# Dilated and sliding-window attention before a fused feed-forward: w3 turned by VectorE, dilated v loaded in place, gates in pairs

## The chip, the cores and the metric

The kernel runs on one core of a Trainium2 chip. The metric is device time in microseconds (us) of one execution, the median of three. The engines are TensorE (PE; its weight loads are shown as PEld), VectorE (DVE), ScalarE (ACT), GpSimd (POOL) and SyncE (SP). GpSimd and SyncE here mostly issue DMA transfers.

## What is computed

q, k and v have 8 batches of 8 heads, 576 positions and 64 columns, in float32. Heads 0 to 3 attend to the last 32 positions, heads 4 to 7 to every fourth of the last 128. The 4,608 rows of 512 columns that result go through a feed-forward with a product in the middle:

```python
mask_plain = (rel >= 0) & (rel < 32)
mask_dil = (rel >= 0) & (rel < 128) & (rel % 4 == 0)
scores = np.where(masks, scale * q @ k.T, -1e9)      # masks: plain for heads 0..3
attn = softmax(scores); x = attn @ v                 # x: (4608, 512)
a = x @ w1; b = x @ w2                               # (4608, 1024)
out = ((a * b) @ w3) @ w_out                         # (4608, 512)
```

The maximum is not subtracted in the kernel. All matrix products take bf16 operands.

## The kernel before

**The fused weight.** (a*b) @ w3 @ w_out is computed as (a*b) @ wf with wf = w3 @ w_out, made once. For the product, each block of 128 rows of w3 (`load_w3`, L323) is turned: eight TensorE transposes of 128x128 (`w3_back`, L644), a copy from PSUM to SBUF by ScalarE (`w3_keep`, L652), eight matmuls with w_out (`w3_mul`, L656), and a cast into `wf_sb` (`w3_done`, L668).

**Attention.** A batch is done in two halves of heads, u = 0 (plain) and u = 1 (dilated), each in six blocks of 96 positions. The dilated heads become the plain pattern by putting positions of equal remainder modulo 4 behind each other, in the order of `RES`. q and k are loaded with a cast to bf16 (`load_rows`, L247) and turned by VectorE's 32x32 transposes of 4-byte words (`turn`, L377). A `Group` (L426) computes the scores of up to five blocks of 4 heads (40 matmuls), ScalarE takes the exponential (L465), VectorE multiplies by the mask (L473). For batches below `BIASED` a group has three blocks, and four matmuls with the identity first add a bias of -30000 outside the window (L437), in place of the mask. A `Step` (L475) multiplies by v with a column of ones (`values`, L482), takes the reciprocal of the ones column (L501) and normalizes (`norm`, L503: one instruction for u = 0, two for u = 1). For batches below `TURNED` TensorE turns the result (`back`, L527) and ScalarE or VectorE copies it to `XT` (`keep`, L536); later batches use a DMA transpose issued by SP.

v must lie with positions on partitions, each block with a halo of 32 earlier positions. For batches 0 and 1 it is turned by VectorE and again by TensorE (`v_back`, L407) and put away by ScalarE or VectorE (`v_keep`, L417). From batch 2 on (`DIRECT_V`) it is loaded in place: the plain heads by one DMA (L286), the dilated ones by eight in rows of 64 numbers, 256 bytes (`load_v_dil`, L291); the halo is copied by VectorE (`halo_v`, L305).

**Feed-forward.** The rows are taken in 16 units of 288. For each unit and each of the 8 blocks f of d_ff, `up` (L559) makes a and b with four matmuls each, `copy_a` (L571) brings a to SBUF by ScalarE, `gate` (L576) multiplies by VectorE into `gt`, a ring of four units. `down` (L585) multiplies 128 rows of the ring by `wf_sb`; `copy_y` and `store` write them out. Thus a `down` needs all eight parts of wf, and unit 4 needs room in the ring.

**The order of the work.** Every step is a `Task` with an engine, an assumed duration, its inputs and a priority (`RANK`, `FIRST`; smaller goes first). `Plan.run` (L80) plays these through in Python, gives every PSUM user one, two or four of the eight banks, and fills empty TensorE time before the first `up` with dummy matmuls (`fill`, L700). The result is a fixed order for each engine; on the chip, each instruction waits for its inputs. The loads form one queue on GpSimd, with at most eight in flight: k, q of batch 0, heads 0 to 3, come by SP in float32 (`load_whole`, L256), then the lists `B0_LOADS` and `FIRST_LOADS` (L40, L45) in their order. In these, "w" is a part of w1 and w2, "3" a block of w3, "o" a half of w_out, and the digits give the part or batch and the half of the heads. `HALVED` and `ON_DVE` say which copies go to which engine; `begin` (L1001) orders the first two units, half of f at a time.

Of the kernel before, what the change touches and what calls it, by code (L numbers as in the profile page):

```python
# [10 lines left out]
P = 128  # L11
# [18 lines left out]
BIASED = 1  # L30
LATE = False
TURNED = 2
# [3 lines left out]
RANK = dict(E=0.5, VK=3, K=2, N=0.2, T=0.5, VT=0.05, S=0.1, V=0.05, X=0.1, W=0.5, C=5)  # L36
FIRST = {"E": 3, "VK": 1, "K": 0.2, "N": 2, "T": 0.2, "VT": 0.05, "S": 0.3, "V": 0.1, "X": 0.3}
WARM = 25
FILL = 110
FIRST_LOADS = ("30", "w0", "v10", "w1", "w2", "31", "k10", "q10", "o0", "o1", "32", "33", "34", "q11", "k11", "v11", "35", "36", "37")  # L40
SHIFT = {}
ON_DVE = ("K0.2", "VK0.1.1", "W3D1", "W3D4", "W3D5")
GRP = 5
WHOLE = ("qn", "kn")
B0_LOADS = ("v0", "q1", "k1", "v1")  # L45
HALVED = ("K0.0", "K0.1", "K0.3", "K1.1", "VK0.0.0", "VK0.1.0", "VK1.0.1", "VK1.1.0")
MASK_AT = 19.5
PARTED = 0
BUSY = 4500
LEAD = 1.1  # L50
# [13 lines left out]
class Plan:  # L64
# [15 lines left out]
    def run(self):  # L80
# [42 lines left out]
        while len(order) < n:  # L123
            progress = True
            while progress:
                progress = False
                for e in engines:
# [8 lines left out]
                    else:  # L136
                        idle = e == "PE" and now >= self.fill_from and self.fill_to.start is None
                        f = Task("fill", "PE", FILL, [], self.fill, 0, 1, 0, ())
# [48 lines left out]
def kernel(  # L187
# [28 lines left out]
    w3_pool = ctx.enter_context(tc.tile_pool(name="w3", bufs=7))  # L216
# [9 lines left out]
        const.tile([P, 2 * B, 2, VC], BF16, name="XT1"),  # L226
# [4 lines left out]
    vps = [const.tile([P, H, 6, PITCH], BF16, name=f"vp{i}") for i in range(2)]  # L231
# [4 lines left out]
    vts = [const.tile([P, 2, PADK + S, 2], BF16, name=f"vt{i}") for i in range(1)]  # L236
# [47 lines left out]
    def load_v_plain(b):  # L284
        flat = vps[b % 2][:, 0:4, :, :].rearrange("p h m e -> p (h m) e")
        nc.gpsimd.dma_start(  # L286
            out=flat[32:P, :, 0:D],
            in_=v_rows(b, 0, 0, [[D, QB], [QB * D, 24], [1, D]]),
        )

    def load_v_dil(b, m):  # L291
        vp = vps[b % 2]
        (r, r2), mu = RES[2 * (m // 3) : 2 * (m // 3) + 2], m % 3
        runs = {
            0: [(0, 96, r, 0)],
            1: [(0, 48, r, 96), (48, 48, r2, 0)],
            2: [(0, 96, r2, 48)],
        }[mu]
        for p0, n, res, t0 in runs:
            nc.gpsimd.dma_start(  # L300
                out=vp[32 + p0 : 32 + p0 + n, 4:8, m, 0:D],
                in_=v_rows(b, 4, 4 * t0 + res, [[4 * D, n], [S * D, 4], [1, D]]),
            )
# [10 lines left out]
    def load_wo(c):  # L314
        g = slice(4 * c, 4 * c + 4)
        nc.gpsimd.dma_start(
            out=wo_sb[:, g, :],
            in_=moe_w_out[512 * c : 512 * (c + 1), :].rearrange("(a p) f -> p a f", p=P),
        )
# [3 lines left out]
    def load_w3(ft):  # L323
        w3n[ft] = w3_pool.tile([P, d_ff], BF16, tag="w3", name="w3n")
        nc.gpsimd.dma_start(out=w3n[ft], in_=moe_w3[ft * P : (ft + 1) * P, :])
# [91 lines left out]
    def v_keep(b, u, half, eng, hs=slice(0, 4)):  # L417
        dst = vps[b % 2][:, 4 * u : 4 * u + 4, 3 * half : 3 * half + 3, 0:D]
# [56 lines left out]
    class Step:  # L475


        def __init__(self, b, u, hf, parts):
            self.b, self.u, self.hf, self.parts = b, u, hf, parts
            self.o = [None, None]  # L480

        def values(self):  # L482
# [3 lines left out]
            self.o = o[:, :, 0 : 3 * (D + 1)].rearrange("p h (m e) -> p h m e", m=3)  # L486
            for g in range(4):
                for mm, (grp, i) in enumerate(self.parts):
                    c0 = (grp.n * g + i) * QB
                    nc.tensor.matmul(  # L490
                        out=self.o[:, g, mm, :],
                        lhsT=grp.et[:, c0 : c0 + P],
                        rhs=vps[self.b % 2][:, 4 * self.u + g, 3 * self.hf + mm, 0 : D + 1],
                        start=True,
                        stop=True,
                    )

        def recip(self):
            self.rcp = wk_pool.tile([P, 4, 3], F32, tag="rcp", bufs=4, name="rcp")
            self.xo = wk_pool.tile([P, 12 * D], BF16, tag="xo", bufs=4, name="xo")  # L500
            nc.vector.reciprocal(out=self.rcp[0:QB, :, :], in_=self.o[0:QB, :, :, D])  # L501

        def norm(self, part):  # L503

            if part is None:
                hs = slice(0, 4)
                dst = self.xo[0:QB, :].rearrange("p (m g d) -> p g m d", m=3, g=4)
            else:
                hs = slice(2 * part, 2 * part + 2)
                dst = self.xo[0:QB, :].rearrange("p (q m g d) -> p q g m d", q=2, m=3, g=2)  # L510
                dst = dst[:, part, :, :, :]
            n = hs.stop - hs.start
            nc.vector.tensor_tensor(  # L513
                out=dst,
                in0=self.o[0:QB, hs, :, 0:D],
                in1=self.rcp[0:QB, hs, :].unsqueeze(3).to_broadcast([QB, n, 3, D]),
# [3 lines left out]
        def cols(self):  # L520

            if self.u == 0:
                m0 = self.b * BLK + 3 * self.hf
                return XT[0][:, m0 : m0 + 3, :, :].rearrange("p m g x -> p (m g x)")
            return XT[1][:, 2 * self.b + self.hf, :, :].rearrange("p g x -> p (g x)")
# [26 lines left out]
    def unit_cols(k, c):  # L552

        b, hf = k // 2, k % 2
        if c < 2:
            return XT[0][:, b * BLK : (b + 1) * BLK, c, 48 * hf : 48 * hf + 48]
        return XT[1][:, k, c - 2, :].rearrange("p (r m t) -> p m r t", r=2, m=BLK)

    def up(k, f, key, chunks=ORDER, first=True, last=True):  # L559
        if first:  # L560
            held[(key, k, f)] = bank(UNIT)
        for j, c in enumerate(chunks):
            nc.tensor.matmul(  # L563
                out=held[(key, k, f)],
                lhsT={"a": w1_sb, "b": w2_sb}[key][:, c, f * P : (f + 1) * P],
                rhs=unit_cols(k, c),
                start=(first and j == 0),
                stop=(last and j == len(chunks) - 1),
            )

    def copy_a(k, f):  # L571
        a_sb = wk_pool.tile([P, UNIT], BF16, tag="asb", bufs=6, name="asb")
        nc.scalar.copy(out=a_sb, in_=held[("a", k, f)])  # L573
        held[("s", k, f)] = a_sb

    def gate(k, f):  # L576
        c0 = (k * UNIT) % RING
        nc.vector.tensor_tensor(  # L578
            out=gt[:, f, c0 : c0 + UNIT].rearrange("p (r m t) -> p m r t", r=2, m=BLK),
            in0=held[("b", k, f)].rearrange("p (m r t) -> p m r t", r=2, m=BLK),  # L580
            in1=held[("s", k, f)].rearrange("p (m r t) -> p m r t", r=2, m=BLK),
# [61 lines left out]

    def w3_back(ft):  # L644
        x = bank(KFF * P, BF16).rearrange("p (g x) -> p g x", g=KFF)
        for g in range(KFF):
            nc.tensor.transpose(  # L647
                out=x[:, g, :], in_=w3n[ft][:, g * P : (g + 1) * P], identity=ident
            )
# [6 lines left out]
    def w3_mul(ft):  # L656
        o = bank(d_model)
        for g in range(KFF):
            nc.tensor.matmul(  # L659
                out=o,  # L660
                lhsT=w3T[ft][:, g, :],
# [28 lines left out]
    def constants():  # L690
        for t in kts + vts:
            nc.vector.memset(t[:, :, 0:PADK, :], 0.0)
        for t in ets:
            for x in (4 * VC, 4 * GRP * QB):
                nc.vector.memset(t[:, x : x + 32], 0.0)
        for t in vps:
# [33 lines left out]
    def loads_v(b):  # L730
        old = vdone.get(b - 2, [])
        LV[b] = [load(f"LP{b}", 1300, 4700, old, lambda: load_v_plain(b))]
        LV[b] += [
            load(f"LD{b}.{m}", 600 if m % 3 != 1 else 1200, 770, old, lambda m=m: load_v_dil(b, m))
            for m in range(6)
# [316 lines left out]
```

## Time and profile before

| | |
|---|---|
| median of 3 runs | 254.95 us (254.93 to 254.96) |
| span of the profiled execution, first to last instruction | 253.2 us |
| around the span (difference to the median) | 1.75 us |
| TensorE busy | 245.8 us |
| VectorE busy | 167.9 us, 350 instructions |
| ScalarE busy | 124.3 us |
| chain of waits, share of TensorE | 90% |
| first product of `up` in the chain | 20.44 us |
| last matmul product of `down` starts | 247.76 us |
| mean granted TensorE clock | 0.998 |

The profile comes from one execution. Matmuls overlap, so the mean time of one matmul in the groups is longer than its share of TensorE; that share is read from the chain of waits, where 12 products of `up` follow each other in 1.47 us. A group's line gives the source line, engine, operation, output and input tiles, shape, count, then busy time, mean ns of one, and the idle time of the engine just before, with what ended it. The profile gives no separate time for the profiled execution beyond its span.

### The profile page before, as it was taken

The page shows a single profiled execution, that of the slowest core. Times are in us where ns is not written, and L with a number is a line of the kernel's source. Part 1 is how long each engine was busy: PE and PEld are TensorE (multiplying, and loading weights), DVE is VectorE, ACT ScalarE, POOL GpSimd, SP SyncE. Part 2 cuts the span into 40 slices and gives each one's busy share as a digit, 9 for nine tenths or more (in the row PEclk, how much of TensorE's full clock was granted, in tenths as well). Part 3 has the DMA queues.
Part 4 walks back from the last instruction along what each step waited for, and adds up shares of the span by engine and source line. Part 5 has one row for each costly group of instructions (what it writes and reads, how often), then busy time and mean ns, then how long its engine had stood idle before and what let it go on. Part 6 is the DMA issues. An engine that isn't in the chain of part 4 may idle for free.

```text
span 253.2 us, 6818 instructions
## 1 busy us (share of the span) xinstructions
PE 245.8 (97%) x2760; PEld 170.6 (67%) x2760; DVE 167.9 (66%) x350; ACT 124.3 (49%) x221; POOL 67.8 (27%) x106
## 2 busy tenths in 40 slices
PE   7889999999999999999999999999999999999994
PEld 5668876565767676677676766676767666777662
DVE  3998657697898887588868977837737365333321
ACT  5664555766635534362626526356353643333331
POOL 7635835343614432303250310800000000000000
PEclk9999999999999999999999999999999999999999
DMA  7999999999997999998799667862332223311114
GB/s 226 204 200 209 207 210 211 208 107 184 220 168 121 189 170 208 235 95 114 122 202 110 89 77 104 137 84 65 67 65 67 67 67 67 104 36 51 41 41 124
DMA packets 59422, 33.40 MB, mean 132 GB/s; under 512 B 44800, under 2 KB 49280, under 8 KB 59392
## 3 DMA queue, kind: packets, MB, share of 16 engines
q0 software_dynamic: 38592, 18.81, 58.7%
q1 hardware_dynamic: 20656, 14.10, 24.3%
q8 instruction: 21, 0.34, 0.6%
q14 instruction: 9, 0.07, 0.1%
q10 hardware_dynamic: 144, 0.07, 0.1%
HBM read 38.80 MB, written 9.44 MB: 190 GB/s over the span
## 4 chain that ended last, share of the span: by engine, by line
PE 90%; DVE 5%; DMA 2%; issue 1%; ACT 1%; ACTq 0%; DVEq 0%
PE ps L563 49%; PE ps L589 24%; PE ps L659 6%; PE ps L490 4%; PE ps L454 4%; DMA gt<-in_q_dram 2%; DVE qt L403 1%; DVE xo L513 1%; PE ps L647 1%; PE ps L607 1%; PE ps L701 1%; PE ps L530 1%; ACT qn L278 0%; DVE et L473 0%; PE ps L412 0%
## 5 line engine op out<-in xcount | busy, mean ns | idle before, releaser
L563 PE MATMUL ps<-XT,w_sb 128*128 128x288 bf16 x1024 | 136.3, 286 | 0.0
L563 PEld LDWEIGHTS <-w_sb 128*128 128x128 bf16 x1024 | 97.8, 98 | 30.6
L578 DVE TENSOR_TENSOR gt<-ps,asb 128x288 bf16<-128x288 f32 x128 | 57.5, 454 | 49.0 <-PE ps L563 46.7
L573 ACT CAST asb<-ps 128x288 bf16<-128x288 f32 x128 | 50.7, 398 | 49.3 <-PE ps L563 46.0
L589 PE MATMUL ps<-wf_sb,gt 128*128 128x512 bf16 x280 | 65.8, 379 | 0.0
L600 ACT COPY osb<-ps 128x512 f32<-128x512 f32 x35 | 20.5, 585 | 55.1 <-PE ps L589 55.0
L589 PEld LDWEIGHTS <-gt 128*128 128x128 bf16 x280 | 27.2, 98 | 26.9
L300 POOL DMA_DIRECT2D vp<-in_v_dram x48 | 30.3, 639 | 48.3 <-PE ps L490 30.3
L465 ACT ACTIVATE et<-ps 128x1920 bf16<-128x1920 f32 (+2 forms) x21 | 34.2, 1633 | 7.7 <-PE ps L454 5.5
L513 DVE TENSOR_TENSOR xo<-ps,rcp 96x384 bf16<-96x384 f32 (+1 forms) x48 | 31.4, 675 | 0.5
L473 DVE TENSOR_TENSOR et<-et,mask 128x960 bf16<-128x960 bf16 (+1 forms) x34 | 21.2, 645 | 6.8 <-ACT et L465 6.7
L403 DVE STREAM_TRANSPOSE qt<-qn 128x320 uint32<-128x320 uint32 (+3 forms) x34 | 22.3, 670 | 2.1 <-ACT qn L278 1.8
L490 PEld LDWEIGHTS <-et 128*128 128x128 bf16 x384 | 14.6, 98 | 1.9 <-issue 0.4
L490 PE MATMUL ps<-vp,et 128*128 128x65 bf16 x384 | 15.5, 193 | 0.1
L659 PE MATMUL ps<-wo_sb,w3T 128*128 128x512 bf16 x64 | 15.0, 379 | 0.1
L403 DVE STREAM_TRANSPOSE kt<-kn 128x320 uint32<-128x320 uint32 (+3 forms) x18 | 11.6, 646 | 4.5 <-PE ps L454 4.3
L454 PEld LDWEIGHTS <-kt 32*128 32x128 bf16 x768 | 9.1, 92 | 5.9 <-issue 4.7
L454 PE MATMUL ps<-qt,kt 32*128 32x96 bf16 x768 | 12.1, 201 | 0.7 <-DVE kt L388 0.7
L501 DVE RECIPROCAL rcp<-ps 96x12 f32<-96x12 f32 x32 | 6.9, 218 | 8.3 <-PE ps L490 8.0
L286 POOL DMA_DIRECT2D vp<-in_v_dram x6 | 7.2, 1194 | 11.5 <-PE ps L490 10.7
L659 PEld LDWEIGHTS <-w3T 128*128 128x128 bf16 x64 | 5.9, 98 | 6.3 <-issue 0.3
L388 DVE STREAM_TRANSPOSE kt<-kn 128x576 uint32<-128x576 uint32 (+1 forms) x9 | 9.9, 1121 | 0.2 <-PE ps L454 0.2
(56 smaller groups left out, 117.6 us busy)
## 6 DMA issues: line engine op xcount, KB each, us to landing
qn<-in_q_dram POOLq DMA_DIRECT2D x6, 576.0 KB, 8.2
kn<-in_k_dram POOLq DMA_DIRECT2D x6, 576.0 KB, 9.0
w3n<-in_moe_w_dram POOLq DMA_DIRECT2D x8, 256.0 KB, 11.2
out_dram<-osb SPq DMA_DIRECT2D x7, 256.0 KB, 3.0
out_dram<-osb SPq DMA_DIRECT2D x8, 224.0 KB, 2.9
vp<-in_v_dram POOLq DMA_DIRECT2D x6, 288.0 KB, 9.2
out_dram<-osb SPq DMA_DIRECT2D x8, 192.0 KB, 2.9
out_dram<-osb SPq DMA_DIRECT2D x8, 160.0 KB, 3.2
```

Source lines behind the costliest of these rows:

```text
L300: nc.gpsimd.dma_start(out=vp[32 + p0 : 32 + p0 + n, 4:8, m, 0:D], in_=v_rows(b, 4, 4 * t0 + res, [[4 * D, n], [S * D, 4], [1, D]]),)
L403: nc.vector.transpose(out=o, in_=i)
L454: nc.tensor.matmul(out=self.sp[:, g, QB * i : QB * i + QB], lhsT=kt[prt, u, QB * m : QB * m + P, c], rhs=qq, start=(c == 0 and not biased) ...
L465: nc.scalar.activation(out=ev, in_=self.sp[:, :, 0:x], func=ACT.Exp, scale=scale)
L473: nc.vector.tensor_tensor(out=ev, in0=ev, in1=mk, op=AL.mult)
L490: nc.tensor.matmul(out=self.o[:, g, mm, :], lhsT=grp.et[:, c0 : c0 + P], rhs=vps[self.b % 2][:, 4 * self.u + g, 3 * self.hf + mm, 0 : D + ...
L513: nc.vector.tensor_tensor(out=dst, in0=self.o[0:QB, hs, :, 0:D], in1=self.rcp[0:QB, hs, :].unsqueeze(3).to_broadcast([QB, n, 3, D]), op=AL ...
L563: nc.tensor.matmul(out=held[(key, k, f)], lhsT={"a": w1_sb, "b": w2_sb}[key][:, c, f * P : (f + 1) * P], rhs=unit_cols(k, c), start=(first ...
L573: nc.scalar.copy(out=a_sb, in_=held[("a", k, f)])
L578: nc.vector.tensor_tensor(out=gt[:, f, c0 : c0 + UNIT].rearrange("p (r m t) -> p m r t", r=2, m=BLK), in0=held[("b", k, f)].rearrange("p ( ...
L589: nc.tensor.matmul(out=y, lhsT=gt[:, f, c0 : c0 + P], rhs=wf_sb[:, f, :], start=(f == 0), stop=(f == KFF - 1),)
L659: nc.tensor.matmul(out=o, lhsT=w3T[ft][:, g, :], rhs=wo_sb[:, g, :], start=(g == 0), stop=(g == KFF - 1),)
```

## The change

- w3 is loaded in four pieces of 256 rows; each piece by four DMAs of 256 columns into 32 partitions each (`load_w3`), in rows of 1,024 bytes. VectorE turns it by one transposing instruction of 512 words for each 128 rows (`w3_turn`); `w3_back` and `w3_keep` are no longer used (`W3_DVE` names all four pieces). `w3_mul` reads every second element of the turned tile. `w_out` is loaded with another assignment of rows to partitions to match.
- v of the dilated heads is loaded in place for all batches, in rows of two positions (128 numbers, 512 bytes), by four DMAs, into tiles `vds` of their own. One row serves two remainders; the first has its ones column ahead of it, the second behind. `halo_v` covers the plain heads only.
- Blocks f are taken in pairs after the first ten (`SINGLE`): `up`, `copy_a` and `gate` work on two neighbouring banks.
- `norm` is one instruction for all heads; `XT` has one layout for both halves.
- `BIASED` is 2 instead of 1. Ranks, the order of the loads (w_out and w3 last), which copies go to which engine, the place of the masks (`MASK_AT`) and `LEAD` are changed. The dummy matmuls are limited to 200.

```diff
-BIASED = 1
+BIASED = 2
+W3_DVE = (0, 1, 2, 3)
+SINGLE = 10
-RANK = dict(E=0.5, VK=3, K=2, N=0.2, T=0.5, VT=0.05, S=0.1, V=0.05, X=0.1, W=0.5, C=5)
-FIRST = {"E": 3, "VK": 1, "K": 0.2, "N": 2, "T": 0.2, "VT": 0.05, "S": 0.3, "V": 0.1, "X": 0.3}
+RANK = dict(E=14.678, VK=10.289, K=0.115, N=1.309, T=1.47, VT=1.262, S=3.624, V=0.444, X=8.99, W=0.183, C=2.862)
+FIRST = dict(E=3.06, VK=0.542, K=2.149, N=1.723, T=5.596, VT=64.744, S=0.678, V=0.475, X=11.212)
-FIRST_LOADS = ("30", "w0", "v10", "w1", "w2", "31", "k10", "q10", "o0", "o1", "32", "33", "34", "q11", "k11", "v11", "35", "36", "37")
+FIRST_LOADS = ('k01', 'v00', 'q01', 'd0', 'v10', 'w0', 'w1', 'q10', 'k10', 'w2', 'q11', 'k11', 'd1', 'o0', 'o1', '33', '32', '31', '30')
-ON_DVE = ("K0.2", "VK0.1.1", "W3D1", "W3D4", "W3D5")
+ON_DVE = ('VK0.0.1', 'VK0.1.1', 'VK1.0.0', 'VK1.1.0', 'W3D5', 'W3D6')
-B0_LOADS = ("v0", "q1", "k1", "v1")
-HALVED = ("K0.0", "K0.1", "K0.3", "K1.1", "VK0.0.0", "VK0.1.0", "VK1.0.1", "VK1.1.0")
-MASK_AT = 19.5
+B0_LOADS = ()
+HALVED = ('K0.2', 'K0.3', 'VK0.1.0', 'VK0.1.1', 'VK1.0.0', 'VK1.1.0')
+MASK_AT = 31.5
-LEAD = 1.1
+LEAD = 1.2
...
+    RUNS = ((0, 32, 96, 0, 0), (1, 0, 80, 0, 64), (1, 80, 48, 2, 0), (2, 0, 128, 2, 16))
+    def load_v_dil(b, i):
+        mu, p0, n, res, t0 = RUNS[i]
+        nc.gpsimd.dma_start(
+            out=vds[b % 2][p0 : p0 + n, :, mu, 16 : 16 + 2 * D],
+            in_=v_rows(b, 4, 4 * t0 + res, [[4 * D, n], [S * D, 4], [1, 2 * D]]),
+        )
...
-            in_=moe_w_out[512 * c : 512 * (c + 1), :].rearrange("(a p) f -> p a f", p=P),
+            in_=moe_w_out.rearrange("(p a) f -> p a f", p=P)[:, g, :],
...
+    def load_w3(pc, g):
...
+        rows = moe_w3[256 * pc : 256 * pc + 256, 256 * g : 256 * g + 256]
+        nc.gpsimd.dma_start(
+            out=w3n[pc][32 * g : 32 * g + 32, :, :], in_=rows.rearrange("(a i) x -> i a x", i=32)
+        )
...
+                    if self.u == 0:
+                        vv = vp[:, g, 3 * self.hf + mm, 0 : D + 1]
+                    else:
+                        vv = vd[:, g, mm, 15 + 65 * self.hf : 80 + 65 * self.hf]
...
+    def copy_a(k, fs):
+        a_sb = wk_pool.tile([P, 2, UNIT], BF16, tag="asb", bufs=3, name="asb")
+        held[("s", k, fs[0])] = a_sb[:, 0 : len(fs), :]
+        nc.scalar.copy(out=held[("s", k, fs[0])], in_=held[("a", k, fs[0])])
+    def gate(k, fs):
+        c0 = (k * UNIT) % RING
         nc.vector.tensor_tensor(
+            out=gt[:, fs[0] : fs[-1] + 1, c0 : c0 + UNIT],
+            in0=held[("b", k, fs[0])],
+            in1=held[("s", k, fs[0])],
             op=AL.mult,
         )
...
+    def w3_turn(ft):
+        w3T[ft] = wk_pool.tile([P, 4, P, 2], BF16, tag="w3T", bufs=3, name="w3T")
+        o = w3T[ft].rearrange("p r f c -> p (r f c)").bitcast(U32)
+        i = w3n[ft // 2][:, 4 * (ft % 2) : 4 * (ft % 2) + 4, :].rearrange("p a x -> p (a x)").bitcast(U32)
+        nc.vector.transpose(
+            out=o.rearrange("p (r a f) -> p r a f", r=4, a=4),
+            in_=i.rearrange("p (a j r) -> p r a j", a=4, r=4),
+        )
...
-                lhsT=w3T[ft][:, g, :],
+                lhsT=w3T[ft][:, g // 2, :, g % 2] if ft // 2 in W3_DVE else w3T[ft][:, g, :],
```

## The prediction

> **What bounds the kernel now.** I read the page first, then the busy time by stretch, TensorE's waits, the chain of waits around the start, and last the groups by shape.
>
> ```profile
> span 253.2 us, 6818 instructions
> PE 245.8 (97%) x2760; PEld 170.6 (67%) x2760; DVE 167.9 (66%) x350; ACT 124.3 (49%) x221; POOL 67.8 (27%) x106
> ```
> ```profile
> 0.00:20.30 20.30, 16.77 (x259) 12.71 (x260) 15.39 (x49) 12.28 (x19) 12.35 (x26) 1.00 1.09 210
> 20.30:58.20 37.90, 37.72 (x415) 26.21 (x413) 27.38 (x52) 22.77 (x37) 18.58 (x27) 1.00 1.21 188
> 58.20:135.00 76.80, 76.80 (x932) 52.77 (x931) 61.70 (x118) 38.46 (x67) 27.77 (x40) 1.00 1.24 168
> ```
> Columns: length, then busy PE, PEld, DVE, ACT, POOL, clock, DMA share, GB/s. After 20.3 TensorE is busy all but 0.2 of 37.9 us and then all of the time. So the kernel has two parts: a start of 20.3 us, set by how early the first product of `up` (L563) can run, and TensorE's own work after it.
>
> ```profile
> 12.02 0.39 DVE vp L424
> 12.41 0.37 DVE vt L403
> 12.80 0.42 DVE vt L403
> 13.26 0.51 PE ps L412 x6
> ...
> 15.73 2.60 DVE xo L513 x4
> ...
> 20.44 1.47 PE ps L563 x12
> ```
> The chain through the start is VectorE's: it was busy 13.45 of the 13.9 us from 6.1 to 20.0, turning q, k and v of batch 0, putting v away, normalizing.
>
> ```profile
> 10.71 0.74 POOL L310 DMA_DIRECT2D w_sb<-in_moe_w_dram  x1 [0.65 <-DMA kn<-in_k_dram]
> 12.06 0.74 POOL L310 DMA_DIRECT2D w_sb<-in_moe_w_dram  x1 [0.61 <-DMA vn<-in_v_dram]
> ...
> 15.67 0.54 POOL L252 DMA_DIRECT2D kn<-in_k_dram  x1 [1.81 <-DMA w_sb<-in_moe_w_dram]
> ```
> The number in brackets is idle time and what ended it: GpSimd issues its n-th load when the (n-8)-th has landed. This dates the landings: k at 10.7, v at 12.05, the first half of w0 by 15.7 us. One half of q, k or v (288 KB as stored in bf16, 590,000 bytes as read in float32) follows another by 1.35 us: 437 GB/s read. A load of 256 KB of weights takes 1.3.
>
> ```profile
> L578 DVE TENSOR_TENSOR gt<-ps,asb 128x288 bf16<-128x288 f32 x128 | 57.5, 454 | 49.0 <-PE ps L563 46.7 <-ACT asb L573 0.8
> L513 DVE TENSOR_TENSOR xo<-ps,rcp 96x384 bf16<-96x384 f32 x32 | 16.5, 543 | 0.3
> L513 DVE TENSOR_TENSOR xo<-ps,rcp 96x768 bf16<-96x768 f32 x16 | 14.9, 938 | 0.3
> L388 DVE STREAM_TRANSPOSE kt<-kn 128x576 uint32<-128x576 uint32 x7 | 8.7, 1240 | 0.2 <-PE ps L454 0.2
> L647 PE MATMUL ps<-ident,w3n 128*128 128x128 bf16 x64 | 4.4, 219 | 0.0
> ```
> A doubled norm costs 938 against 2 x 543 ns: an instruction has a fixed part near 150 ns. The 219 ns of L647 overlap; the chain shows 16 of them in 0.90 us.
>
> **What the Trainium skill says.** "SBUF — State Buffer", section Door 1: a transfer into partitions 0..31 reaches 8 of 16 ports and was measured at 189 GB/s, one into 128 at 328. No transfer of this kind is in the trace. "DMA: Bandwidth & Descriptors", Specifications, asks for at least 512 B per descriptor; the page's count of 44,800 of 59,422 packets under 512 B shows how far this kernel is from it. "ScalarE: Activation LUTs", section What ACT_TABLE_LOAD costs, gives 186 ns + 0.833 ns an element; the trace agrees in slope (398 ns at 288, 585 at 512 columns: 0.835), with a fixed part of 158, which I use.
>
> **The change part by part.** TensorE's prices come from the chain of waits: product 0.1225 us (12 in 1.47), transpose 0.056 (16 in 0.90), bias product of 288 columns as the product.
>
> 1. *w3 turned by VectorE.* 64 transposes go. Eight of them ran at 13.7 us, in the start, where TensorE had room; 56 x 0.056 = **-3.15 us** count. ScalarE loses 8 copies of 1.03 us. VectorE gains 8 transposes of 512 words, 2.15 ns each by L388: 1.1 us, 8.9 in all. Its input steps by 16 bytes, which no row shows: between 1.1 and 2.3 us each; I take 1.15. It is hidden while TensorE has other work.
> 2. *v of the dilated heads loaded in place.* For batch 1, 12 of 24 transposes go: **-0.67 us**; for batch 0 they lay in the start. On VectorE, before the first product, 1.82 us of turning dilated v (12.3 to 15.2 us) and 2.05 us of putting v away go; the change puts 0.95 back (one whole `v_keep`), moves 0.75 of `keep` to ScalarE, and joins two norms (-0.15). Net -3.8 us.
> 3. *BIASED = 2.* Batch 1 takes 16 bias products: +1.96 us, and has 4 groups of scores instead of 2.4; the first product behind a group takes 0.1 us longer (1.58 against 1.47), +0.16. **+2.1 us**. VectorE loses 2.4 groups x 2 masks x 0.65 = 3.1 us.
> 4. *Gates of two blocks.* 59 pairs after 10 single ones: a gate pair 154 + 2 x 300 = 754 ns against 908, a copy pair 158 + 480 = 638 against 796. That frees 9 us on each engine, at cover: TensorE waits for neither now, so 0. Risk: a pair holds two PSUM banks for some 1.9 us each. By bank-time (2 banks x (0.98 + 0.1 + 0.64 or 0.75 + 0.1) for a and b, 4 x 2.7 for scores, 2 x 1.8 for values, 1 x 2.5 for down) I get about 111 of 213 bank-us in a batch: enough. Bounds 0 to +1.5 us; I take 0.3.
> 5. *Single norm, halo of 4 heads, fewer loads of v:* VectorE and GpSimd only, both with slack. 0. The odd start of a value column (element 15 or 80) is not in the trace: 384 values matmuls at 30 ns; 0 to +1 us for the 192 dilated ones; I take 0.
> 6. *Weights as every second element* (`w3_mul`): the v transposes load every second element now, in 98 ns as all others. 0.
> 7. *Order of loads.* By the dated landings, k01 7.8, v00 9.3, q01 10.7; d0 has 1,408 rows of 512 B, 0.72 MB: 1.65 us at the full rate, and 3.3 at half of it; I take 2.9, so 13.6. v10 15.0, w0 (two) 17.8, w1 20.4, q10 and k10 23.2, w2 28.4, q11 and k11 31.2, d1 34.1, w_out 39.1, w3 49.5. The first product then waits for w0, at **18.0**, not for VectorE (20.3 - 3.8 = 16.5, with copies on ScalarE perhaps 17.5). w0 feeds 4 products, 1.96 us, to 20.0; w1 comes at 20.4: -2.3 + 0.4 = **-1.9 us**. w2 at 28.4: TensorE has until then the first halves of units 0 and 1 (7.8 us), the rest of batch 0 (0.65), and v and scores of batch 1's first half (2.3): 29.2. Hidden, by 0.8.
> 8. *w_out and w3 last.* `down` needs all of w3's products. TensorE has without them units 0 to 3 (31.4 us) and batch 1 (6 us), until 55; its 64 w3 products (13.8 us) fit between 42 and 56. w3 lands at 49.5, if quadrants move at the full rate. From the skill's 189 GB/s, an estimate: since half of the bytes read are written, 378 GB/s read, 11.1 us for 4.2 MB against 10.4, so 0.7 later. I charge 0.3. SP's queue is not passed by any of this. GpSimd issues 16 loads of w3 instead of 8 (0.54 us each), and its masks (4.75 us at 24.0) go behind later loads, since batch 1 needs none now; it waits for landings anyway (12.35 of 20.3 us busy). Behind w3 on its queue come the loads of batch 2, needed only when nine `down`s (15.6 us) have run out.
>
> VectorE between 18 and 58 us: gates of units 0 to 3 12.8 (10 x 0.454 + 11 x 0.754), batch 1 11.8 (turns of q, k and v 6.6, putting v away 0.6, four reciprocals and norms 4.6), w3 9.2 and two casts of its products 1.4, one norm left of batch 0 1.2, the start of batch 2 about 5: 41.4 us for 40. It fills up (27.4 of 37.9 now). That is the cover which items 1 and 4 lean on: if the transposes take 2.3 us it is gone by 9 us, but half of batch 2 can still wait behind the `down`s.
>
> Sum: -3.15 - 0.67 + 2.1 - 1.9 + 0.3 + 0.3 = -3.0 us on the span: 250.2. What lies around it is 254.95 - 253.2 = 1.75, and the runs spread by 0.03. So **252.0 us**.
>
> **The rivals.**
> *Nothing gained at the start.* d0 in 512-byte rows is slower than 3.3 us, or w1 and w2 are awaited: then only TensorE's work counts, -1.7: 253.2 (252.8 to 254.3). For it: w0 and w2 come with less than 1 us to spare. Against: the rows are twice as long as those of the old loads.
> *A larger gain.* d0 moves at the full rate: w0 at 16.6, first product 17.0, and no loss to banks: 254.95 - 1.7 - 3.4 = 249.8.
> *Slower: quadrants.* Each w3 load fills 32 partitions. TensorE runs in a fixed order; if the w3 products are placed for loads at the old rate, each waits until its quadrants are in, and everything behind it. At 1.5 times the time (4.8 us late, the stall on TensorE) 252 + 4.8 = **256.8**; it turns to slower from 3.1 us of lateness, a third over the old rate. For it: the 189 GB/s. Against: writes are half of the reads.
>
> **How the numbers follow.** Forecast 0.56 (250.6 to 253.0), nothing at the start 0.14, larger gain 0.08, within 0.2% 0.05 (banks and lateness eat 3 us), slower 0.17. Faster 0.78, same 0.05, slower 0.17; 0.2%, 0.5 us, is about what a measurement can tell from no change. Range 249.7 to 255.8: half of the larger gain and most of the slower case stay out.
>
> **What would show it.** Right: the first L563 product at 18.0, waiting for w_sb; no idle TensorE behind it; L647 gone and 16 more bias products; gates of 0.75 us; w3 transposes of 1.15 us. Wrong: TensorE waiting for w3's turns or for w_sb between 20 and 55, w3 landing after 52, pairs waiting for VectorE or ScalarE, or transposes of 2 us.

## The result and the profile after

| | before | after |
|---|---|---|
| median of 12 runs, us | 254.97 (254.89 to 255.06) | 254.54 (254.15 to 258.19) |
| span of the profiled execution, us | 253.2 | 252.9 |
| its own time, us | not given | 254.63 |
| first product of `up` starts, us | 20.27 | 19.16 |
| last part of `down` (256 columns) starts, us | 247.60 | 247.22 |
| TensorE idle from 20.3 to 135 us | 0.18 | 2.77 |

The ratio, with its 95% interval in brackets, is 0.9985 [0.9973, 0.9996]: 0.4 us faster, where 3.0 was forecast. It leaves out the slow run of the kernel after (258.19 us, mean clock 0.987); the other eleven lie between 254.15 and 255.97, 1.8 us apart, where those of the kernel before lie 0.17 apart.

The first two lines of the page:

```profile
span 252.9 us, 6390 instructions
PE 243.7 (96%) x2694; PEld 167.7 (66%) x2694; DVE 158.4 (63%) x270; ACT 109.5 (43%) x154; POOL 62.3 (25%) x96
```

TensorE has 2.1 us less to do, VectorE 9.5, ScalarE 14.8. The page alone would suggest a gain of 2 us. The busy time by stretch (length, then busy PE, PEld, DVE, ACT and POOL, clock, DMA share, GB/s), over the same stretches as before, says where it went:

```profile
0.00:20.30 20.30, 17.68 (x266) 13.60 (x267) 15.52 (x47) 12.45 (x19) 14.15 (x29) 1.00 1.15 207
20.30:58.20 37.90, 37.01 (x400) 25.44 (x398) 27.42 (x45) 16.49 (x29) 22.69 (x35) 1.00 1.25 182
58.20:135.00 76.80, 74.92 (x891) 50.09 (x889) 60.25 (x94) 35.37 (x44) 19.01 (x25) 1.00 1.39 178
```

Subtract the PE column from the length. Before, that left 0.18 and 0.00 us in the second and third stretch; now it leaves 0.89 and 1.88. TensorE, which hardly waited behind the start, waits. In the second stretch VectorE is as busy as before (27.42 against 27.38 of 37.9 us), so it hasn't filled up.

What TensorE waits for (us in all, times, longest):

```profile
PE ps L467 <- ACT osb L611: 1.7, 1, 1.7
...
PE ps L509 <- ACT et L478: 0.7, 2, 0.4
PE ps L467 <- DVE kt L401: 0.4, 1, 0.4
PE ps L537 <- DVE xo L523: 0.4, 1, 0.4
```

One wait makes up most of it: scores (L467) that wait for a copy of an output tile (L611) on ScalarE. A score doesn't read that copy; it waits because the copy frees a PSUM bank. But the copy takes 0.59 us and the wait 1.7, so something holds the copy. The chain of waits around it (start, length, what):

```profile
68.76 0.67 DVE et L486
69.44 0.46 SPq L550
...
69.95 9.88 DMA out_dram<-osb
...
79.90 0.59 ACT osb L611
...
80.54 0.62 PE ps L467 x40
```

A store of an output tile was issued at 69.95 and took 9.88 us. The copy at 79.90 writes into the SBUF buffer that this store was reading. ScalarE's copies and the scores (timeline; in brackets the idle time before, and what ended it):

```profile
69.08 0.59 ACT L611 COPY osb<-ps 128x512 f32<-128x512 f32 x1 [0.41 <-PE ps L600]
70.80 0.59 ACT L611 COPY osb<-ps 128x512 f32<-128x512 f32 x1 [1.14 <-PE ps L600]
73.27 0.59 ACT L611 COPY osb<-ps 128x512 f32<-128x512 f32 x1 [1.88 <-PE ps L600]
...
79.90 0.59 ACT L611 COPY osb<-ps 128x512 f32<-128x512 f32 x1 [2.26 <-DMA out_dram<-osb]
80.38 0.65 ACT L585 CAST asb<-ps 128x576 bf16<-128x576 f32 x1
...
80.54 0.62 PE L467 MATMUL ps<-qt,kt 32*128 32x96 bf16 x40 [1.66 <-ACT osb L611]
```

So four output tiles were due between 69.1 and 79.9 us, and there are three `osb` buffers. ScalarE stood before the fourth copy from 77.64 on (2.26 us), and the copy of a pair (`copy_a`, L585), with its two banks held, stood behind it in ScalarE's queue. The scores came next in TensorE's fixed order and waited for the bank that the output copy frees.

Before, no copy of an output tile waited for a store. Of its seven copies between 62.7 and 91.0 us, five had idle time ahead of them, ended by TensorE each time. The view of `osb` from 60 to 96 us, first before, then after (the copies; what the engine waited for; how long the stores took):

```profile
L600 ACT COPY osb<-ps x7: 585/585/585, 62.7 to 91.0; 128x512 f32<-128x512 f32 x7
...
  PE ps L589: 7.0, 5
...
DMA to landing us min/median/max: 2.9/6.0/7.8
...
L611 ACT COPY osb<-ps x8: 586/586/604, 69.1 to 94.8; 128x512 f32<-128x512 f32 x8
...
  PE ps L600: 4.5, 4
  DMA out_dram<-osb: 2.3, 1
...
DMA to landing us min/median/max: 3.3/7.4/9.9
```

Two things bring the tiles and the slow stores together. The first `down` starts at 67.15 us instead of 60.79, since w_out and w3 now come last and the last part of wf is copied at 66.3. And the stores take longer (a median of 7.4 us against 6.0), while the loads of the next batches share the DMA engines with them.

Why w3 is so late is seen on GpSimd, which issues its loads (L336; L380 makes the masks):

```profile
36.03 4.76 POOL L380 TENSOR_SCALAR mask<-bias 128x384 bf16<-128x384 bf16 x5
40.74 2.89 POOL L336 DMA_DIRECT2D w3n<-in_moe_w_dram  x5
...
49.09 2.42 POOL L336 DMA_DIRECT2D w3n<-in_moe_w_dram  x4 [4.01 <-DVE w3T L659]
```

Nine of the 16 loads of w3 are issued behind the masks, and the last four wait 4.0 us more for one of the three w3 buffers. These four take 6.2 to 6.5 us, so w3 is complete at about 57 us.

The start (timeline: start, length, engine, operation; in brackets the idle time before it and what ended it):

```profile
17.07 1.13 ACT L478 ACTIVATE et<-ps 128x1152 bf16<-128x1152 f32 x1 [1.33 <-PE ps L467]
17.18 0.54 POOL L256 DMA_DIRECT2D kn<-in_k_dram  x1 [0.58 <-DMA w_sb<-in_moe_w_dram]
...
18.09 0.94 ACT L545 COPY XT<-ps 128x576 bf16<-128x576 bf16 x2
18.12 0.50 PE L425 MATMUL ps<-ident,vt 128*128 128x128 bf16 x6
...
18.46 0.53 PE L509 MATMUL ps<-vd,et 128*128 128x65 bf16 x12
...
18.82 0.50 PE L425 MATMUL ps<-ident,vt 128*128 128x128 bf16 x6
```

The load at 17.18 waited for the second part of w0, which dates that landing: 17.2 (forecast 17.8). The first product comes at 19.16, so w0 isn't what it waits for. ScalarE does an exponential and then two copies of `XT` until 19.03, and TensorE's fixed order puts batch 1's turning of v (L425) and the last values step of batch 0 (L509) ahead of the product.

### The profile page after: what moved, and what is told of

Read it like the earlier page. It is cut to its first block, busy times and chain, and to the rows that moved or that the text cites. A ratio compares the mean times of both kernels' runs of the same rounds, so it can differ in the third digit from the quotient of the medians.

```text
span 252.9 us, 6390 instructions
## 1 busy us (share of the span) xinstructions
PE 243.7 (96%) x2694; PEld 167.7 (66%) x2694; DVE 158.4 (63%) x270; ACT 109.5 (43%) x154; POOL 62.3 (25%) x96
## 4 chain that ended last, share of the span: by engine, by line
PE 78%; DMA 18%; ACT 1%; issue 1%; POOL 0%; DVE 0%; SPq 0%; ACTq 0%; POOLq 0%; DVEq 0%
PE ps L574 44%; PE ps L600 21%; PE ps L679 5%; DMA kn<-in_k_dram 5%; DMA out_dram<-osb 4%; PE ps L509 3%; DMA w_sb<-in_moe_w_dram 3%; PE ps L467 3%; DMA vn<-in_v_dram 3%; DMA w3n<-in_moe_w_dram 3%; ACT et L478 1%; PE ps L618 1%; DVE et L486 0%; ACT asb L585 0%; ACT osb L611 0%
## 5 line engine op out<-in xcount | busy, mean ns | idle before, releaser
L589 DVE TENSOR_TENSOR gt<-ps,asb 128x576 bf16<-128x576 f32 (+1 forms) x69 | 49.2, 712 | 62.1 <-PE ps L574 56.2
L585 ACT CAST asb<-ps 128x576 bf16<-128x576 f32 (+1 forms) x69 | 41.7, 605 | 66.9 <-PE ps L574 65.2
L600 PE MATMUL ps<-wf_sb,gt 128*128 128x512 bf16 x280 | 65.7, 379 | 0.0
L600 PEld LDWEIGHTS <-gt 128*128 128x128 bf16 x280 | 27.1, 98 | 26.9
L611 ACT COPY osb<-ps 128x512 f32<-128x512 f32 x35 | 20.4, 587 | 50.6 <-PE ps L600 48.0
L301 POOL DMA_DIRECT2D vd<-in_v_dram x32 | 21.2, 672 | 47.9 <-PE ps L509 43.3
L523 DVE TENSOR_TENSOR xo<-ps,rcp 96x768 bf16<-96x768 f32 x32 | 30.1, 949 | 0.7
L486 DVE TENSOR_TENSOR et<-et,mask 128x960 bf16<-128x960 bf16 (+1 forms) x30 | 17.7, 629 | 0.3 <-ACT et L478 0.2
L509 PEld LDWEIGHTS <-et 128*128 128x128 bf16 x384 | 14.2, 98 | 2.9 <-ACT et L478 1.6
L467 PE MATMUL ps<-qt,kt 32*128 32x96 bf16 x768 | 12.5, 201 | 2.1 <-ACT osb L611 1.7
L467 PEld LDWEIGHTS <-kt 32*128 32x128 bf16 x768 | 9.3, 92 | 7.7 <-issue 6.8
L679 PE MATMUL ps<-wo_sb,w3T 128*128 128x512 bf16 x64 | 14.1, 379 | 0.0
L290 POOL DMA_DIRECT2D vp<-in_v_dram x6 | 7.2, 1197 | 22.2 <-PE ps L509 16.1
L336 POOL DMA_DIRECT2D w3n<-in_moe_w_dram x16 | 9.3, 584 | 7.5 <-DVE w3T L659 4.0
```

Of the source, the lines that this page charges most:

```text
L301: nc.gpsimd.dma_start(out=vds[b % 2][p0 : p0 + n, :, mu, 16 : 16 + 2 * D], in_=v_rows(b, 4, 4 * t0 + res, [[4 * D, n], [S * D, 4], [1, 2 * ...
L467: nc.tensor.matmul(out=self.sp[:, g, QB * i : QB * i + QB], lhsT=kt[prt, u, QB * m : QB * m + P, c], rhs=qq, start=(c == 0 and not biased) ...
L509: nc.tensor.matmul(out=self.o[:, g, mm, :], lhsT=grp.et[:, c0 : c0 + P], rhs=vv, start=True, stop=True,)
L523: nc.vector.tensor_tensor(out=self.xo[0:QB, :].rearrange("p (m g d) -> p g m d", m=3, g=4), in0=self.o[0:QB, :, :, self.val : self.val + D ...
L585: nc.scalar.copy(out=held[("s", k, fs[0])], in_=held[("a", k, fs[0])])
L589: nc.vector.tensor_tensor(out=gt[:, fs[0] : fs[-1] + 1, c0 : c0 + UNIT], in0=held[("b", k, fs[0])], in1=held[("s", k, fs[0])], op=AL.mult,)
```

## The experiments

The kernel before, timed beside these kernels, took 254.98 us in each group, and each ratio is to it. The theory: the store wait costs the 1.7 us. The rivals: the banks that pairs hold, the order of the w3 loads, the start.

**Five output buffers instead of three**, all instructions and their order as in the kernel after:

```diff
-        o_sb = wk_pool.tile([P, d_model], F32, tag="osb", bufs=3, name="osb")
+        o_sb = wk_pool.tile([P, d_model], F32, tag="osb", bufs=5, name="osb")
```

> The changed kernel with 5 instead of 3 output buffers (osb), the order of all instructions as it was. Theory (store wait): ScalarE's copy of the fourth output tile waits at 79.9 us for the first store, which took 9.9 us to land; the copy of a product stands behind it, and TensorE waits 1.7 us for banks. With free buffers this wait is gone: 252.8 to 253.0 us, and a narrower spread of runs. Rival (congestion): the DMA engines are full there, and TensorE will wait for the turned rows of batch 2 instead, or for later loads: 254.2 or more.

Measured: 253.15 us (253.02 to 255.99), ratio to before 0.9933 [0.992, 0.9945]. The profile is of an execution of 255.99 us. The same kernel once more:

> The changed kernel with 5 output buffers once more, since its first profile was taken in an execution in which TensorE waited 2.6 us near 9 us and then ran at half its clock for 4 us. Theory (store wait): 252.8 to 253.3 again, no wait of TensorE over 0.5 us behind 20 us. Rival (the first measurement was a chance): 254 or more.

Measured: 253.10 us (253.03 to 254.64), 0.9938 [0.992, 0.9956], with a profile of 253.09. The stores in it are no quicker (one tile's view, 60 to 96 us):

```profile
DMA to landing us min/median/max: 6.5/8.7/10.9
```

but the copy and the scores come on time (timeline):

```profile
77.52 0.59 ACT L611 COPY osb<-ps 128x512 f32<-128x512 f32 x1
...
78.79 0.61 PE L467 MATMUL ps<-qt,kt 32*128 32x96 bf16 x40
```

The scores start 1.75 us earlier than at 80.54, the span is 1.6 us shorter, the median 1.4. The latency of a store is hidden by buffers, not shortened: with the wait gone, the same stores take longer than ever. This version beats both kernels. It gains 1.9 of the 3.0 us that were forecast, so the wait for the store explains about half of the miss.

The first profile, of 255.99 us, shows what one late load costs. k of batch 0 landed late, and ScalarE's cast of it waited:

```profile
8.88 1.25 ACT L282 CAST kn<-gt 128x576 bf16<-128x576 f32 x2 [2.82 <-DMA gt<-in_k_dram]
...
22.07 1.63 PE L574 MATMUL ps<-XT,w_sb 128*128 128x288 bf16 x12
```

(two parts of its timeline). TensorE waited 2.57 us for kt, the clock was 0.50 from 11 to 13 us and 0.75 from 13 to 15, and the first product came at 22.07 instead of 19.14: 2.93 us later, and the times are 2.90 apart. Why k landed late is not known from these runs.

**No pairs** (`SINGLE = 9999`), three buffers:

```diff
-SINGLE = 10
+SINGLE = 9999
```

> The changed kernel with all blocks f single, no pairs: 128 copies of 400 ns and 128 gates of 454 ns, one bank each. Theory: pairs cost TensorE nothing and gain it nothing, since neither engine is awaited apart from the wait for the store: 254.0 to 255.0. Rival (banks): the pairs' two banks are what makes TensorE wait at 78.9 us; with single blocks the wait of 1.7 us is gone: about 253.0. Third: ScalarE and VectorE need the 9 us each that the pairs free: over 255.5.

Measured: 254.11 us (253.79 to 257.52), 0.9981 [0.9961, 1.0001]. The store wait on ScalarE is still there, but TensorE works through it (timeline):

```profile
79.21 1.89 PE L600 MATMUL ps<-wf_sb,gt 128*128 128x512 bf16 x8
79.75 0.59 ACT L611 COPY osb<-ps 128x512 f32<-128x512 f32 x1 [1.37 <-DMA out_dram<-osb]
```

TensorE is idle for 0.45 us between 76 and 95, against 1.88 in the kernel after. So a copy that waits for a store is not enough for the stall. That the rest is the two banks of a pair is not shown: without pairs the order of the work is another one too, with a `down` (L600) in the place of the scores. Nor is the time clearly lower: the ratio is 0.9981, that of the kernel after 0.9985, and their intervals overlap. What TensorE gains here it mostly loses elsewhere.

**Both: five buffers, no pairs.**

> The changed kernel with 5 output buffers and all blocks f single. Theory: both edits take away the same wait at 79 us, so they don't add: 252.8 to 253.3, as with the buffers alone (253.15). Rival (pairs cost TensorE by themselves, through banks): lower than 252.6. Third (pairs do pay elsewhere): 253.6 or more.

Measured: 253.86 us, 0.9964 [0.9949, 0.9979]. This is the third case: with five buffers, pairs are better by 0.7 us. Where they gain it is not shown; no trace of an execution near this time was kept.

**Four buffers for w3 instead of three.** GpSimd waits 4.0 us before the last four pieces of w3 (`w3n L336 <- DVE w3T L659: 4.0` in its waits), and the loads behind come bunched. A fourth buffer takes that wait away:

```diff
-    w3_pool = ctx.enter_context(tc.tile_pool(name="w3", bufs=3))
+    w3_pool = ctx.enter_context(tc.tile_pool(name="w3", bufs=4))
```

> The changed kernel with a fourth buffer for the pieces of w3, so that the loads of the fourth piece no longer wait 4.0 us on GpSimd's queue for VectorE's first turns; order of instructions as it was. Theory (loads bunched): v of batch 2 and q and k of batch 3 stand behind that wait; 4 us earlier they are out of the way of the first stores at 70 us, the store's 9.9 us get shorter, and TensorE's wait of 1.7 us shrinks: 253.3 to 254.2. Rival: the loads only fill the engines earlier, the store waits as before: 254.4 or more.

Measured: 254.71 us (254.0 to 257.08), 1.0002 [0.9986, 1.0018]. TensorE still waits 1.7 us for the `osb` copy, and the stores take 3.9/7.1/9.9 us (least, median, most). So the 4.0 us on GpSimd aren't the cause. Whether bunched loads are is left open: the loads behind came no earlier, q of batch 3 at 58.03 us against 57.33, since they now waited for other things.

**The start: copies of `XT` earlier**, one of them moved to VectorE:

```diff
-FIRST = dict(... V=0.475, X=11.212)
+FIRST = dict(... V=0.475, X=0.1)
-ON_DVE = ('VK0.0.1', ...)
+ON_DVE = ('K0.2', 'VK0.0.1', ...)
-HALVED = ('K0.2', 'K0.3', ...)
+HALVED = ('K0.3', ...)
```

> The changed kernel with the turning back of a normalized step ahead of the next scores at the start, and the copy of step 0.2 wholly on VectorE, so that ScalarE has one copy less behind its fourth exponential. Theory: the first product of up at 19.16 us waits for ScalarE's copies, not for w0, which had landed by 17.2; it starts at 18.6 or before, and the time is 0.4 to 0.6 us lower, about 254.0. Rival (weights): w1 lands only at 19.8, and what is gained at the first product is lost at the third block: under 0.2 us.

Measured: 255.14 us (253.67 to 258.18), 1.0002 [0.9987, 1.0016]. The copies are done by 18.28, 0.75 us earlier, and the first product comes later, at 19.86: the new order on TensorE has batch 1's transposes and a values step ahead of it all the same, and the bank given to the product is one that `v_keep` still reads (a wait of 0.5). So the copies alone are not the gate; what was placed ahead of the first product is. The store wait stayed (2.0). Neither case of the expectation came: w1's lateness was not tested, since the first product itself came later.

**w3 turned by TensorE again**, with five buffers:

```diff
-W3_DVE = (0, 1, 2, 3)
+W3_DVE = ()
```

> The changed kernel with 5 output buffers, and w3 loaded in whole rows, turned by TensorE and copied by ScalarE as before (the part w3 by VectorE undone). Theory: 64 transposes of 0.056 us come back onto a TensorE that has no idle time, so 253.15 + 3.6 = 256.5 to 257.0. Rival: the idle 0.9 us between 19 and 58 us and the slack of the start take a part, and VectorE's 8.7 us freed shorten waits: 254.5 to 255.5.

Measured: 257.97 us (257.92 to 258.01), 1.0117 [1.0103, 1.013], 4.8 more than with VectorE. 64 transposes at 0.056 are 3.6; the rest is near a wait of 1.1 us at 63.74, where products wait for a bank that ScalarE's second exponential in a row frees. Since the order of the work changed with the edit, the 4.8 is the price of this whole arrangement, not of the transposes alone.

**w3 loaded in the middle again**, with the new pieces, three output buffers:

```diff
-FIRST_LOADS = (..., 'w0', 'w1', 'q10', 'k10', 'w2', 'q11', 'k11', 'd1', 'o0', 'o1', '33', '32', '31', '30')
+FIRST_LOADS = (..., 'w0', 'w1', '33', 'q10', 'k10', 'w2', 'o0', 'o1', '32', 'q11', 'k11', 'd1', '31', '30')
```

> The changed kernel with w_out and half of w3 loaded between batch 1's first and second half of q and k, as in the kernel before, instead of last; 3 output buffers. Theory (late w3 bunches the first stores with the loads of batches 2 and 3): the first down starts near 62 us instead of 67, stores are spread, ScalarE no longer waits for a store, 1.7 us less at 79 us, but batch 1 comes later and TensorE waits for it between 35 and 50 us by about as much: 253.5 to 255. Rival (the order of loads is worth nothing either way): 254.5 with the wait at 79 us as it is.

Measured: 258.41 us (257.4 to 258.88), 1.0128 [1.0112, 1.0144]. TensorE waits 2.2 us for kt, 1.9 of it in one piece between 28 and 31 us, and the clock falls to 0.50 from 32 to 34. Both parts of the theory's mechanism are there. The first `down` starts at 62.87 us, and no output copy waits for a store, though the stores take 5.1/7.1/7.8 us. So with earlier outputs the stall doesn't come. But the delay of batch 1 costs more than was expected: "w3 last" is worth 3.9 us here, as it brings batch 1 in time.

**One biased batch instead of two**, with five buffers (masks early again, since batch 1 needs them):

```diff
-BIASED = 2
+BIASED = 1
-MASK_AT = 31.5
+MASK_AT = 19.5
```

> The changed kernel with 5 output buffers, batch 1 with masks by VectorE in groups of five again (BIASED = 1, masks made earlier). Theory by TensorE's work: 16 bias products and the extra groups fall away, 2.1 us: 251.1. Rival: the bias buys an early and short way through batch 1's attention; groups of five need both halves' q and k, masks add 0.65 us each in VectorE, TensorE runs out of products before unit 2: 254 to 257.

Measured: 265.91 us (263.2 to 268.9), 1.0386 [1.0353, 1.042]: by the ratios about 11.5 us slower than with two, beyond both cases. Less TensorE work, but the way through batch 1 now has larger groups and a VectorE step, and TensorE waits for the masked exponentials (3.1 us in all), for `xo` (2.0) and, near 98 us, for the turned `XT` of a later batch (2.1). By stretch:

```profile
28.00:30.10 2.10, 0.12 (x1) 0.00 (x0) 1.11 (x3) 1.35 (x1) 1.04 (x2) 1.00 1.38 185
30.10:32.00 1.90, 1.62 (x17) 1.16 (x18) 1.31 (x4) 0.00 (x0) 1.23 (x3) 0.69 1.59 213
32.00:34.00 2.00, 2.00 (x11) 1.30 (x10) 1.23 (x3) 0.40 (x1) 1.64 (x3) 0.50 1.06 209
```

2.0 us without a product, and the clock column then falls to 0.69 and 0.50: busy 2.00 of 2.00 us at half the clock is half the work. The column falls to 0.50 twice more, near 48 and 101 us, behind other such waits.

**The bias alone, on the kernel before** (`BIASED = 2`, nothing else):

```diff
-BIASED = 1
+BIASED = 2
```

> The kernel before with BIASED = 2 alone. Theory by TensorE's work: 16 bias products and groups of three, 2.1 us more where TensorE has no idle time: 257.0. Rival (a shorter way through batch 1's attention is worth something by itself, as undoing it in the changed kernel cost 12 us): 255.0 or less.

Measured: 257.70 us (257.6 to 257.71), 1.0105 [1.0092, 1.0118]: 2.7 us slower. The theory holds, but not all of it is TensorE's work. Two waits for an exponential behind a biased group are new (TensorE's timeline):

```profile
37.66 0.54 PE L490 MATMUL ps<-vp,et 128*128 128x65 bf16 x12 [0.26 <-ACT et L465]
...
50.40 0.83 PE L412 MATMUL ps<-ident,vt 128*128 128x128 bf16 x12 [0.27 <-ACT et L465]
```

Without them, 2.2 us are left, near the 2.1 of the sum.

**Dilated v in place alone, on the kernel before**, for batches 0 and 1 in the old rows of 256 bytes:

```diff
-FIRST_LOADS = ("30", "w0", "v10", ..., "q11", "k11", "v11", ...)
+FIRST_LOADS = ("d0", "30", "w0", "v10", ..., "q11", "k11", "d1", ...)
-B0_LOADS = ("v0", "q1", "k1", "v1")
+B0_LOADS = ("v0", "q1", "k1")
+                hal = add(f"HALO{b}", "DVE", 480, LVd[b] + [c0], lambda b=b: halo_dil(b), ...)
```

> The kernel before with one part of the change: dilated v of batches 0 and 1 loaded in place, in the old rows of 256 bytes by eight loads and a halo copy; all else as it was. Theory (my steps 2 and 7): TensorE loses 24 transposes, 0.7 us of them behind the start, VectorE 1.8 us of turning and about 2 us of copies in the start; the first product comes 1 us or more earlier: 253.0 to 253.8. Rival (weights): eight loads of 256-byte rows push w0 back to about 19 us, and nothing is gained at the start: 254.3 to 255.5.

Measured: 262.98 us (260.87 to 263.79), 1.0296 [1.0261, 1.0331]. The first product does come earlier, at 19.40, with VectorE relieved; but the DMA moves 173 GB/s in the first 19 us instead of 210, and batch 1 comes late: TensorE waits 1.7 us for masked exponentials. Near 99 us it waits 2.4 us for the turned `XT` of a later batch. Alone this part doesn't pay. Which of the rows of 512 bytes, the order of loads and the bias it needs was not separated.

**w2 earlier**, with five buffers (ahead of q and k of batch 1):

```diff
-FIRST_LOADS = (..., 'w1', 'q10', 'k10', 'w2', 'q11', ...)
+FIRST_LOADS = (..., 'w1', 'w2', 'q10', 'k10', 'q11', ...)
```

> The changed kernel with 5 output buffers and w2 loaded before q and k of batch 1's first half. Theory: w2 landed at 27.9 us, and TensorE, out of products, waited 0.9 us in pieces between 29 and 31 us for exponentials and norms of batch 1; with w2 at 25.3 these waits go, but batch 1 comes 2.7 us later and the waits move to it, with a risk of a longer one near 34 us: 252.7 to 254. Rival (order is balanced to the microsecond): over 255, with an idle stretch of 1.5 us or more and a lower clock behind it.

Measured: 255.20 us (255.08 to 256.88), 1.0028 [1.0016, 1.0041], 2.1 more than with five buffers alone. TensorE now waits for batch 1: 1.9 us for exponentials and 1.0 for `xo`, against 0.9 and 0.4 with five buffers alone. In 38 to 58 us it is busy for 18.45 of 20, against 19.68, and in 58 to 76 for 16.95 of 18, against 17.84. The time is the rival's, without a wait of 1.5 us. w2 where it was is the better place.

## Why the prediction was right in direction and wrong in size

The sum, term by term, on the span:

| term | forecast | measured | from |
|---|---|---|---|
| w3's transposes go | -3.15 | -3.15 | L647 is gone |
| dilated v of batch 1 | -0.67 | -0.67 | 12 transposes fewer |
| second biased batch | +2.1 | +2.7 | run of the bias alone, 0.5 of it waits |
| start | -1.9 | -1.8 | first product 1.1 earlier, 0.7 of batch 1's transposes ahead of it |
| waits behind the start | +0.6 | +2.6 | TensorE idle 2.77 less 0.18 |
| sum | -3.0 | -0.3 | measured: -0.43 in the medians, -0.3 in the span |

The first two rows are counts at the same price, not timed by themselves. The waits of 0.5 us in the third row have their like in the kernel after (0.26 us at 29.03 and at 38.63), which the last row counts again. So it is partly luck that the rows meet the span. Of the rivals none came as it was put; the case that did, "banks and lateness eat 3 us", had no place named for it.

**The step that failed is step 8**, "w_out and w3 last", with its charge of 0.3 and its sentence "SP's queue is not passed by any of this". I followed the moved loads to those who need w3 and looked at the queue in which stores are issued. I didn't follow the start of the `down`s to the stores and their three buffers. The trace of before had what was needed: stores of up to 7.8 us in that stretch, and tiles a few us apart. Without the wait the fourth copy comes at 77.52, 7.6 us after the first store's issue at 69.95: that is all the cover that three buffers give, and the store took 9.88. Undone by buffers alone, this is worth 1.4 us.

The same step also dated w3 wrongly: forecast 49.5, complete at about 57. "Go behind later loads" was said of the masks, and "it waits for landings anyway", so they were charged nothing; they stand ahead of nine loads of w3 and take 4.76 us. From 41 to 42 us the core moved only 45 GB/s, with few loads under way. "w3 landing after 52" was my own sign of being wrong, and it came. No product of w3 on TensorE waited for a load, as the rival "quadrants" had it; the fixed order has the last of them at 62.84, and that is what moved the outputs. How many of the 6.4 us by which the first `down` is later come from the masks was not tested.

**The second piece, 0.9 us, is a term that step 7 left out.** w2 had landed by 27.98 (forecast 28.4), and TensorE didn't wait for it: "Hidden, by 0.8" held. But TensorE waits for batch 1's exponentials and norms: 0.26 us before 29.03, 0.36 before 30.95, 0.26 before 38.63 (the last is put down to a landing of w3 in this trace, to an exponential in the one with five buffers). The cover was counted in work, but that work is itself a chain through ScalarE and VectorE with steps of about 1 us (1.13 for the exponential of a biased group). TensorE's order is fixed, so the products that w2 allows stand behind it, at 29.41. A reordering of the loads moved this wait (w2 earlier: +2.1) and didn't remove it.

**The third is step 3.** In the run with five buffers, a biased group of scores takes 0.96 us from start to start (four bias products 0.59, 24 scores 0.37: 26.75, 27.34, 27.71); I had priced its bias products at 0.49. A group of 40 without bias takes 0.55 (80.54 to 81.09). Four of the one against 2.4 of the other are 3.84 - 1.32 = 2.5. With the two waits of 0.5 us that makes 3.0, and 2.7 was measured. So the miss of 0.6 holds waits, which I had at nothing, and dearer bias products; the two were not weighed apart. But the bias had another use that I gave no value: as its removal showed (+11.5), it keeps batch 1 short enough to be ready in time.

**The start came out at the right size for a wrong reason.** I took w0 to be the gate, at 18.0; it landed at 17.2. The order on TensorE and ScalarE was the gate. Batch 1's transposes, placed ahead of the first product, would have come behind it anyway, as in the kernel before (at 23.47). So part of what looks like a late start is work done early; in the sum it is 1.1 + 0.7. That this meets the forecast of 1.9 is luck.

**What was right.** VectorE's transposes, the doubled gate and copy, and the odd start of the values' columns (groups by shape: count, busy us, mean ns, idle before):

```profile
L589 DVE TENSOR_TENSOR gt<-ps,asb 128x576 bf16<-128x576 f32 x59 | 44.6, 756 | 61.0 <-PE ps L574 56.2 <-ACT et L478 3.3 <-ACT XT L545 0.6
L585 ACT CAST asb<-ps 128x576 bf16<-128x576 f32 x59 | 37.7, 639 | 62.8 <-PE ps L574 62.4 <-DVE et L486 0.3
...
L659 DVE STREAM_TRANSPOSE w3T<-w3n 128x512 uint32<-128x512 uint32 x8 | 8.6, 1084 | 0.6 <-PE ps L679 0.6
L509 PE MATMUL ps<-vd,et 128*128 128x65 bf16 x192 | 8.2, 194 | 0.7 <-ACT et L478 0.4 <-DMA w3n<-in_moe_w_dram 0.3
L509 PE MATMUL ps<-vp,et 128*128 128x65 bf16 x192 | 8.0, 193 | 0.3 <-ACT et L478 0.3
```

A pair's gate takes 756 ns (forecast 754), its copy 639 (638), a transpose of w3 1,084 (1,150, with the steps of 16 bytes at no cost). The values from `vd`, at an odd column, take 194 ns, those from `vp` 193. The rival "slower: quadrants" didn't happen: no product of w3 waited for a load. But the pieces do move more slowly than other loads. Where w3's packets of 512 bytes make up nearly all traffic, the core moves 194 GB/s (36 to 40 us), 118 (42 to 47) and 188 (53 to 56). From 32 to 35.5 us, when the larger rows of w_out come in, it moves 213. Pieces for all four quadrants were under way together, so this neither confirms nor refutes the 189 GB/s of the Trainium skill ("SBUF — State Buffer", section Door 1), and why 42 to 47 us is slower still was not taken apart. Banks were in my list of risks at 0.3 us, but as pairs alone; with five buffers pairs gain 0.7 us, and with a late store TensorE waits 1.7, whose share due to the banks is open.

**Open.** Which loads make the first store take 9.9 us was not taken apart. Five output buffers on the kernel before weren't tried. That none of ScalarE's output copies waits for a store there speaks against a gain. With five buffers the kernel is still 1.1 us above the forecast of 252.0, and none of these runs removes the waits for batch 1.

## What to carry to other kernels

When a change moves the time at which outputs begin, price the outputs too: tiles due, buffers, and the landing time of a store in that stretch, not over the whole run; then ask who stands behind the copy in its engine's queue and which banks it holds. When an engine that never waited gets less work, the gain is real only if it still never waits: subtract its busy time from each stretch before and after. A cover counted in TensorE's work can itself hold waits, if that work is a chain through other engines and the order is fixed. Where an engine issues loads and does other work too, look at which loads stand behind that work.

## What the hardware showed that I had not expected

- Some 2 us without a product can halve TensorE's clock for a while: idle 28.0 to 30.1, then 0.69, 0.50 and 0.94 in the next three stretches of about 2 us (one biased batch); idle about 2 us in 28.0 to 30.8, then 0.64, 0.50, 0.86 (w3 in the middle). An estimate from these columns: the clock's shortfall adds about 1.7 us to such a wait. But a wait of 2.44 us that ended at 99.70 (dilated v alone) left the clock at 1.00, as did the 1.66 us of the kernel after. So the length of the wait alone doesn't decide it. The Trainium skill, "TensorE: Matmul & The Clock Gate", section Part 1: The HAM clock gate, gives one idle window of about 3.4 us for this; in the first two cases less was enough.
- Stores of 32 to 256 KB, which take 2.0 to 3.4 us by the page's medians over the whole run, took up to 9.9 (kernel after) and 10.9 (five buffers) beside the loads.
- A weight operand of every second element (turned w3) and a moving operand that starts at an odd element cost nothing that the trace shows (98 ns a weight load; 194 against 193 ns).
